# Windowed attention with a squared-ReLU feed-forward: from the fifth token tile on, tiles in pairs and Strassen's seven products in the first feed-forward matmul, with weights streamed from DRAM

## The chip, the core and the metric

The kernel runs on one core of a Trainium2 chip. The metric is the device time of one execution in microseconds; the kernel before takes 879.53 us, the median of 3 runs (877.98 to 879.83). Work is spread over TensorE (PE), VectorE (DVE), ScalarE (ACT), GpSimd (POOL) and SyncE (SP, which here only issues DMAs).

## The reference, cut to what matters

```
scores = q @ k.T / sqrt(64)            # 8 batches, 8 heads, 576 tokens, head size 64
scores = where(0 <= i - j < 64, scores, -1e9)
attn   = exp(scores - max); attn /= attn.sum() + 1e-9
x = (attn @ v), heads side by side     # 4608 tokens x 512
h = x @ w_in                           # 512 x 2048
g = max(h, 0) ** 2
out = g @ w_out                        # 2048 x 512
```

Weights arrive as 64-bit floats, so a weight row is twice as long in DRAM as in fp32.

## The kernel before

The 4608 tokens are cut into 12 tiles of 384. A feed-forward tile goes over 16 blocks `f` of 128 hidden units. For each block `mm1` (line 346) makes h, 128 units x 384 tokens, in 12 matmuls of 384 columns: 4 chunks of the model dimension, times 3 because fp32 accuracy is put together from two rounded halves (weight-hi x x-hi, weight-hi x x-lo, weight-lo x x-hi). `evac` then applies ReLU on ACT (op r), squares on DVE (p), rounds to the high half on ACT (g) and subtracts to the low half on DVE (G). `mm2` (line 387) follows two blocks later with 9 matmuls of 512 columns (3 token blocks x 3 halves) that add into three PSUM banks. One such step of mm1 and mm2 is the unit of the PE's work; a tile has 16.

The weights stay in SBUF for the whole run: `weight` (line 83) turns each 64-bit block into the two halves in the first stage, and all 16 blocks (`wparts`, 8 KB per partition each) stay there. Tiles 0 and 1 run interleaved in the first stage, by an order written out by hand (line 475), while weights load and convert. From line 541 on tiles 2 to 11 run one after another.

Attention for the next tile runs beside the feed-forward, in 36 sections of 4 query blocks, three to a tile. `section` (line 194) does one: S scores (PE), o and s copy and mask, z max, e and f exponentials (ACT), m normalise (POOL), X transpose (PE), x mask (DVE), V values (PE), H and Q the two halves of x. `step` (line 430) puts S of section i and V of section i-1 on the PE between an mm1 and an mm2. Queries and keys come as `raw` tiles: `load_qk` (line 114) issues 8 DMAs of 72 KB, whose runs in DRAM are 32 numbers long, into one of two buffers; `turn` (line 138) transposes a raw tile into `qk` on DVE, behind the last S that reads the old one, and the next load into that buffer waits for it. `load_v` (line 125) issues 64 KB DMAs into `vt`. Each engine takes its instructions strictly in the order in which the code emits them; all DMAs are issued by SP in one such queue. After a tile, ACT copies the three banks to `osb` (put Z, line 408) and SP writes them out (put W, line 410).

Of the kernel before, what the change touches and what calls it, by code (L numbers as in the profile page):

```python
# [20 lines left out]
NEG = -1.0e30  # L21


@with_exitstack
def window_attention_relu2_ffn(ctx: ExitStack, tc: tile.TileContext, q, k, v, w_in, w_out, out):
# [15 lines left out]
    wpool = ctx.enter_context(tc.tile_pool(name="wpool", bufs=NF))  # L41
    wst = ctx.enter_context(tc.tile_pool(name="wst", bufs=2))
    dram = ctx.enter_context(tc.tile_pool(name="dram", bufs=1, space=bass.MemoryType.DRAM))
    att = ctx.enter_context(tc.tile_pool(name="att", bufs=2))
    ffn = ctx.enter_context(tc.tile_pool(name="ffn", bufs=2))
    ps_a = ctx.enter_context(tc.tile_pool(name="ps_a", bufs=1, space=bass.MemoryType.PSUM))
    ps_h = ctx.enter_context(tc.tile_pool(name="ps_h", bufs=1, space=bass.MemoryType.PSUM))
    ps_o = ctx.enter_context(tc.tile_pool(name="ps_o", bufs=1, space=bass.MemoryType.PSUM))
# [65 lines left out]
    def load_qk(b, g):  # L114
        raw = raws[b, g] = att.tile([P, 2, S], F32, name="raw", bufs=2)
        for hd in range(2):
            for e in range(2):
                r = slice(32 * (2 * hd + e), 32 * (2 * hd + e) + 32)
                for n, x in enumerate((q, k)):
                    y = x[b, 4 * (g % 2) + 2 * (g // 2) + hd].rearrange("(t i) (e l) -> e i t l", i=32, e=2)[e]  # L120
                    sp.dma_start(raw[r, n].rearrange("i (t l) -> i t l", l=32), y)
# [3 lines left out]
    def load_v(b, t):  # L125
        vt = vts[b, t] = att.tile([P, 2, H // 2, D], F32, name="vt", bufs=5)
# [6 lines left out]
    def get_turned(b, d):  # L133
        if (b, d) not in turned:
            turned[b, d] = att.tile([P, 2, 2, S], F32, name="qk", bufs=2)
# [25 lines left out]
    def turn_first(b, t, d):  # L161
        n = tokens(b, t)
        early = b == 0 and 0 < 2 * t + d < 3
        ps = ps_o.tile([P, 2, 2, P], F32, name="oV" if early else "oT", bufs=2 if early else 1)
# [15 lines left out]
    def sel_tile(i):  # L180
        if i < 6 and i % 4 > 1:
            return extra[:, i % 2 * 512:(i % 2 + 1) * 512].rearrange("p (w h c) -> p w h c", w=SW, h=2)
        return att.tile([P, SW, 2, QB], F32, name="sel")

    def pt_tile(i):
        if i < 6 and i % 2:
            return extra[:, 1024:].rearrange("p (w q) -> p w q", q=P)
        return att.tile([P, 2 * SW, P], F32, name="pt", bufs=1)
# [5 lines left out]
    def section(op, i, eng=None):  # L194
# [3 lines left out]
        if op == "S":  # L198
            ps = ps_s[i] = ps_a.tile([P, 2, SW * P], F32, name="s_ps")
# [10 lines left out]
            nms[i] = att.tile([P, SW * 2], F32, name="nm", bufs=3)  # L210
            sums[i] = att.tile([P, SW * 2], F32, name="sums", bufs=3)
# [28 lines left out]
        elif op == "R":  # L240
            rs[i] = att.tile([P, SW * 2], F32, name="rs", bufs=3)
# [4 lines left out]
        elif op == "X":  # L246
            ps_t[i] = (ps_o.tile([P, SW * P], F32, name="oV", bufs=2) if i < 3 else
                       ps_a.tile([P, 2, SW * P], F32, name="v_ps")[:, 0]).rearrange("p (w q) -> p w q", w=SW)
# [8 lines left out]
        elif op == "V":  # L257

            ps = ps_x[i] = ps_a.tile([P, 2, SW * P], F32, name="v_ps")
# [17 lines left out]
        else:  # L277
            hi, lo = (x.rearrange("p (m d) x -> p m d x", d=2) for x in get_x(i // SPT))
# [43 lines left out]

    def get_x(t):
        if t not in xt:
            xt[t] = (ffn.tile([P, NPAIR, TT], F32R, name="xhi"), ffn.tile([P, NPAIR, TT], F32R, name="xlo"))
        return xt[t]
# [19 lines left out]
    def mm1(t, f):  # L346
        xhi, xlo = get_x(t)
        h_ps = ps_h.tile([P, TT], F32, name="h_ps")
        n = 0
        for kk in range(NK):  # L350
            for part, xx in ((0, xhi), (0, xlo), (1, xhi)):
                pe.matmul(h_ps, lhsT=wparts[f][:, 0, part, kk * P:(kk + 1) * P], rhs=in_turn(xx[:, kk, :]),  # L352
# [5 lines left out]
    def evac(op, n, eng=None):  # L358
        if op == "r":
            rg[n] = ffn.tile([P, TT], F32, name="r")  # L360
# [6 lines left out]
        elif op == "g":  # L367
            gs[n] = (ffn.tile([P, TT], F32R, name="ghi", bufs=3), ffn.tile([P, TT], F32R, name="glo", bufs=2))
# [15 lines left out]
    hs, rg, gs, accs = {}, {}, {}, {}  # L384


    def mm2(t, f, ghi, glo):
        if f == 0 and t == 1:
            accs[t] = [ps_a.tile([P, 2, SW * P], F32, name=x)[:, n] for x, n in (("s_ps", slice(0, 2)), ("v_ps", 0))]
            accs[t] = [accs[t][0][:, 0], accs[t][0][:, 1], accs[t][1]]  # L390
        elif f == 0:
            accs[t] = [ps_o.tile([P, DM], F32, name="oV" if tb else "oT", bufs=2 if tb else 1) for tb in range(NTB)]
        for tb in range(NTB):
            ts = slice(tb * P, (tb + 1) * P)
            for n, (gg, part) in enumerate(((ghi, 0), (ghi, 1), (glo, 0))):
                pe.matmul(accs[t][tb], lhsT=gg[:, ts], rhs=in_turn(wparts[f][:, 1, part, :]),  # L396
                          start=f == 0 and n == 0, stop=f == NF - 1 and n == 2)
            if f == NF - 1 and t != 1:
                for op in "ZW":
                    put(op, t, tb)  # L400
# [4 lines left out]
    def put(op, t, tb):  # L405
        if op == "Z":
            outs[t, tb] = wst.tile([P, DM], F32, name="osb", bufs=3)
            act.copy(by_half(outs[t, tb]), ordered(accs[t][tb]))
# [21 lines left out]
    def step(n, i, slot):  # L430
        if slot == 0:
            section("S", i)
            section("V", i - 1)
            evac("p", n)
            section("o", i)
            section("s", i)
            section("H", i - 1)
            evac("g", n)
            section("z", i)
            section("y", i, "d")  # L440
            section("e", i)
            section("Q", i - 1)
            evac("G", n)
            section("f", i)
            if i in loads:
                do_load_v(loads[i])
        elif slot == 1:
            section("k", i, "d")
            section("R", i)
            section("m", i)  # L450
# [5 lines left out]

# [126 lines left out]
```

## Time and profile before

| | |
|---|---|
| runs | 877.98 to 879.83 us, median 879.53 |
| profiled execution: span | 878.4 us (the page gives no other time for it) |
| PE busy | 860.0 us, 98% |
| weight loads of PE | 794.7 us, 90% |
| DVE busy | 452.0 us, 51% |
| ACT busy | 401.8 us, 46% |
| POOL busy | 50.1 us, 6% |
| DMA moved | 56.41 MB, 64 GB/s over the span |

In the profile a group's row has the line, the engine, the operation, the tiles (out<-in), the shape, the count, the busy time and the mean of one, and what ended the idle time before. A matmul's duration covers its pipeline, so the pace of the PE is read from the starts of its rows in time and not from their lengths. `SPq` rows are DMAs being issued. A row of the view by windows has the stretch and its length, then the busy time and the count of each engine, then the granted TensorE clock, the mean busy share of the 16 DMA engines and GB/s.

### The profile page before, as it was taken

Reading aid. Unit: us, or ns where it says so; the run is one execution under the profiler, and the core shown is the slowest. Engines: PE = TensorE matmul, PEld = TensorE weight load, DVE = VectorE, ACT = ScalarE, POOL = GpSimd, SP = SyncE. Lnnn points to the kernel's source line nnn. Section 1 sums busy time; section 2 is a strip of 40 time slices with the busy share of each in tenths; the row PEclk is TensorE's granted clock in tenths of the full one; section 3 lists DMA queues with packets and bytes.
Section 4 is the critical chain, followed back from the end, with each engine's and each line's share of the span. In section 5 each row is a group of like instructions: output and inputs, shape, how many; then the busy total and the mean of one; then the engine's idle time right before and its main releaser. Section 6 shows DMA issues by size and latency. Waiting matters only on the chain.

```text
span 878.4 us, 16976 instructions
## 1 busy us (share of the span) xinstructions
PE 860.0 (98%) x6946; PEld 794.7 (90%) x6946; DVE 452.0 (51%) x740; ACT 401.8 (46%) x1147; POOL 50.1 (6%) x70
## 2 busy tenths in 40 slices
PE   6799999999999999999999999999999999999998
PEld 5688998899999999999999999999999999999997
DVE  5799995754455444544455444453445544432222
ACT  5787875644344434434334444334434443432322
POOL 1210000210000000000000000000000000000000
PEclk9899999999999999999999999999999999999999
DMA  9989206460125002421033202141013200100100
GB/s 213 222 270 327 37 4 106 81 155 7 26 55 121 1 1 64 71 48 54 1 55 92 54 2 63 29 81 55 11 21 67 59 1 1 37 1 1 37 1 36
DMA packets 200302, 56.41 MB, mean 64 GB/s; under 512 B 185377, under 2 KB 193569, under 8 KB 200225
## 3 DMA queue, kind: packets, MB, share of 16 engines
q1 hardware_dynamic: 200224, 55.34, 27.4%
q8 instruction: 54, 0.88, 0.4%
q14 instruction: 24, 0.19, 0.1%
HBM read 45.88 MB, written 9.44 MB: 63 GB/s over the span
## 4 chain that ended last, share of the span: by engine, by line
PE 94%; SPq 3%; DMA 1%; ACT 1%; POOL 0%; DVE 0%; issue 0%; POOLq 0%
PE h_ps L352 42%; PE oV L396 26%; PE oT L396 14%; PE s_ps L208 3%; PE v_ps L272 3%; PE s_ps L396 2%; PE v_ps L250 1%; SPq L158 1%; PE v_ps L396 1%; SPq L130 1%; DMA w<-in_k_dram 1%; PE h_ps L500 0%; ACT sel L236 0%; SPq L80 0%; ACT r L361 0%
## 5 line engine op out<-in xcount | busy, mean ns | idle before, releaser
L352 PE MATMUL h_ps<-xhi,w 128*128 128x384 f32 x1536 | 407.0, 327 | 1.9 <-ACT r L361 1.4
L352 PEld LDWEIGHTS h_ps<-xhi,w 128*128 128x128 f32 x1536 | 275.2, 189 | 8.6 <-ACT r L361 3.3
L352 PE MATMUL h_ps<-xlo,w 128*128 128x384 f32 x768 | 250.6, 326 | 0.0
L361 ACT ACTIVATE r<-h_ps 128x384 f32<-128x384 f32 x192 | 93.6, 487 | 286.4 <-PE h_ps L352 285.7
L396 PE MATMUL oV<-w,ghi 128*128 128x512 f32 x704 | 209.5, 379 | 0.0
L366 DVE TENSOR_TENSOR r<-r 128x384 f32<-128x384 f32 x166 | 92.0, 554 | 165.4 <-ACT r L361 165.4
L371 DVE TENSOR_TENSOR glo<-r,ghi 128x384 fp32r<-128x384 f32 x192 | 107.8, 562 | 121.0 <-PE oV L396 82.0
L369 ACT CAST ghi<-r 128x384 fp32r<-128x384 f32 x192 | 98.8, 514 | 117.4 <-DVE r L366 115.4
L396 PEld LDWEIGHTS oV<-w,ghi 128*128 128x128 f32 x704 | 133.2, 189 | 18.8
L352 PEld LDWEIGHTS h_ps<-xlo,w 128*128 128x128 f32 x768 | 145.3, 189 | 4.8
L396 PE MATMUL oV<-w,glo 128*128 128x512 f32 x352 | 133.5, 379 | 0.0
L396 PE MATMUL oT<-w,ghi 128*128 128x512 f32 x352 | 110.2, 395 | 0.0
L236 ACT ACTIVATE sel<-sel,nm 128x64 f32<-128x64 f32 x272 | 90.8, 335 | 17.4 <-DVE nm L230 15.3
L396 PEld LDWEIGHTS oV<-w,glo 128*128 128x128 f32 x352 | 66.6, 189 | 9.4
L245 POOL TENSOR_TENSOR sel<-sel,rs 128x512 f32<-128x512 f32 x33 | 38.4, 1163 | 564.4 <-DVE rs L242 564.4
L396 PE MATMUL oT<-w,glo 128*128 128x512 f32 x176 | 66.8, 379 | 0.0
L254 DVE TENSOR_TENSOR pt<-v_ps,masks 128x1024 f32<-128x1024 f32 x31 | 38.0, 1224 | 46.8 <-PE v_ps L250 46.8
L396 PEld LDWEIGHTS oT<-w,ghi 128*128 128x128 f32 x352 | 59.0, 189 | 2.3 <-issue 0.2
L236 ACT ACTIVATION_READ_ACCUMULATOR sel<-sel,nm 128x1 f32 x272 | 50.9, 187 | 0.0
L140 DVE STREAM_TRANSPOSE qk<-raw 128x1152 f32<-128x1152 f32 x28 | 38.4, 1371 | 1.4 <-issue 1.4
L208 PE MATMUL s_ps<-qk 64*64 64x128 f32 (+1 forms) x1104 | 38.3, 276 | 0.1
L396 PEld LDWEIGHTS oT<-w,glo 128*128 128x128 f32 x176 | 33.3, 189 | 4.7
(80 smaller groups left out, 592.6 us busy)
## 6 DMA issues: line engine op xcount, KB each, us to landing
vt<-in_v_dram SPq DMA_DIRECT2D x144, 64.0 KB, 2.5
out_dram<-osb SPq DMA_DIRECT2D x36, 256.0 KB, 2.3
w<-in_moe_w_in_dram SPq DMA_DIRECT2D x16, 512.0 KB, 6.6
w<-in_moe_w_out_dram SPq DMA_DIRECT2D x16, 512.0 KB, 7.6
raw<-in_q_dram SPq DMA_DIRECT2D x112, 72.0 KB, 2.5
raw<-in_k_dram SPq DMA_DIRECT2D x112, 72.0 KB, 2.5
w<-in_q_dram SPq DMA_DIRECT2D x5, 256.0 KB, 4.6
w<-in_k_dram SPq DMA_DIRECT2D x5, 256.0 KB, 5.2
```

What stands on the lines that cost most here:

```text
L140: dve.transpose(get_turned(b, g // 2)[:, g % 2].rearrange("p n t -> p (n t)"), raw.rearrange("p n t -> p (n t)"))
L208: pe.matmul(ps[half * QB:(half + 1) * QB, j, w * P + c0:(w + 1) * P], lhsT=qk[r, 0, qb * QB:(qb + 1) * QB], rhs=qk[r, 1, k0:k0 + P - c0], ...
L236: act.activation(sels[i][:, w, hd], sels[i][:, w, hd], AF.Exp, bias=nms[i][:, n], scale=SCALE, accum_out=sums[i][:, n])
L245: (dve if eng == "d" else pool).tensor_tensor(p, p, rs[i][:, :, None].broadcast_to([P, SW * 2, QB]), ALU.mult)
L254: dve.tensor_tensor(pts[i].rearrange("p (w n) q -> p w n q", n=2), ps_t[i][:, :, None, :].broadcast_to([P, SW, 2, P]), masks.rearrange("p ...
L272: pe.matmul(ps[hd * D:(hd + 1) * D, j, q0:q0 + n * QB], lhsT=vts[b, kb // 2][r, kb % 2, 2 * d + hd, :], rhs=pts[i][r, n0:n0 + n, half * QB ...
L352: pe.matmul(h_ps, lhsT=wparts[f][:, 0, part, kk * P:(kk + 1) * P], rhs=in_turn(xx[:, kk, :]), start=n == 0, stop=n == 3 * NK - 1)
L361: act.activation(by_half(rg[n]), ordered(hs.pop(n)), AF.Relu)
L366: dve.tensor_tensor(rg[n], rg[n], rg[n], ALU.mult)
L369: act.copy(gs[n][0], rg[n])
L371: dve.tensor_tensor(gs[n][1], rg.pop(n), gs[n][0].bitcast(F32), ALU.subtract)
L396: pe.matmul(accs[t][tb], lhsT=gg[:, ts], rhs=in_turn(wparts[f][:, 1, part, :]), start=f == 0 and n == 0, stop=f == NF - 1 and n == 2)
```

## The change

The first stage stays, with three additions. Fixed buffers and PSUM banks replace the pools. Two more steps (tile 2, blocks 0 and 1) go into the hand-written order. Each converted weight block is also written to DRAM (`kept`, token B: 16 DMAs of 1 MB).

After the first stage the weight tiles are released and their space goes to new buffers. Weights come back from `kept` by DMA: `wi` blocks of 256 KB (half of an mm1 block, both roundings; 12 slots), `wo` blocks of 512 KB (an mm2 block; 8 slots). Tiles 2 and 3 run as before but with streamed weights: 30 more steps, two `wi` and one `wo` for each. In the same stretch the attention of tiles 4 and 5 is finished (9 sections instead of 6), and `mix` builds on POOL, for each pair p of blocks f, the four sums of weight quarters that Strassen's products need, and writes them to DRAM (`mixed`, 1 MB per p, 8 in all).

Tiles 4 to 11 run as 4 pairs j. The token half (first or second tile of the pair), the half of the model dimension and the block of a pair of f form the 2 x 2 x 2 cases. `operands` builds 7 combinations of the x quarters (POOL, DVE) and rounds each into two halves (ACT, DVE). Step s (8 per pair of tiles, 32 in all) does 7 products of 6 matmuls each where mm1 took 8 x 6: products 0 to 3 start four PSUM banks, products 4, 5 and 6 add into the banks of products 1, 2 and 3, after DVE has taken the first value out (`add` to v, u and g22). `second(s-2, x)` then does mm2 for four blocks f at once: 12 matmuls for each of 3 token blocks, whose result DVE adds to `part` in SBUF.

The order of the instructions on each engine from tile 2 on is no longer written by the loops but by `Plan`: each operation is entered with its engine, a cost, what it reads and writes and, for a DMA, a time to land; `in_order` lays them out by when they could start, the least late first, with PE in the order of entry. A DMA of weights is entered at 0.1 us of SP, `load_qk` (8 DMAs) at 0.8, one `load_v` at 0.4; transfers don't compete in it.

```
+NWI = 12
+NWO = 8
+NPLAIN = 4
...
+            elif op == "B":
+                sp.dma_start(kept[n], wparts[n].bitcast(F32))
...
+    wst.release()
+    wpool.release()
+    strm = ctx.enter_context(tc.tile_pool(name="strm", bufs=1, reuse_waits="tile"))
+    wi_t = [strm.tile([P, 2, 2, 2 * P], F32R, name=f"wi{n}") for n in range(NWI // 2)]
...
+        plan("sp", 0.1, by(sp.dma_start, wi[name][0].bitcast(F32), source), keys, [wi[name][1]], 3.5)
...
+        plan("sp", 0.1, by(sp.dma_start, wo[name][0].bitcast(F32), kept[f, :, 1]), [], [wo[name][1]], 5.0)
...
+                    plan("dve", 1.4, by(turn, b, g), [("raw", g % 2)], [("qk", g // 2, g % 2)])
...
+                    plan("sp", 0.8, by(load_qk, b, g), [], [("raw", g % 2)], 3.0)
...
+    def mix(p, n):
...
+        plan("sp", 0.1, by(sp.dma_start, mixed[p], mx.bitcast(F32)), ["mx0", "mx1"], [("mixed", p)], 4.0)
...
+    def product(s, n):
+        p = s % NP
+        kind = (0, "A11", 2, 3, "A12", "A22", 1)[n]
+        source = mixed[p, :, kind] if isinstance(kind, int) else block(2 * p + (kind[1] == "2"), int(kind[2]) - 1)
+        wi_fetch((s, n, "s"), source, [("mixed", p)] if isinstance(kind, int) else [])
+        w, w_key = wi[s, n, "s"]
+        if n < 4:
+            sums_of[s, n] = bank()
+        ps, key = sums_of[s, (0, 1, 2, 3, 1, 2, 3)[n]]
+        x = ops_x[n]
+
+        def do():
+            m = 0
+            for kk in range(2):
+                for part, xx in ((0, 0), (0, 1), (1, 0)):
+                    pe.matmul(ps[:, :TT], lhsT=w[:, part, kk * P:(kk + 1) * P], rhs=in_turn(x[:, xx, kk]),
+                              start=n < 4 and m == 0, stop=m == 5, skip_group_check=True)
+                    m += 1
...
+        if n == 0:
+            plan("act", 0.5, by(act.copy, sc, b[0][:, :TT]), [b[1]], ["sc"])
+        elif n == 1:
+            add(v, [kv], a[0][:, :TT], a[1], sc, "sc")
+        elif n == 2:
+            add(u, [ku], c[0][:, :TT], c[1], v, kv)
+        elif n == 3:
+            add(by_half(g22[0]), g22[1] + used, ordered(d[0][:, :TT]), d[1], ordered(u), ku)
+            square(g22, False, SQUARES[0])
...
+    def second(k, x):
...
+            for m in range(4):
+                for n, (gg, part) in enumerate(((hi, 0), (hi, 1), (lo, 0))):
+                    pe.matmul(ps, lhsT=gg[:, m // 2, m % 2], rhs=in_turn(w[m][0][:, part]),
+                              start=m == 0 and n == 0, stop=m == 3 and n == 2)
...
+            plan("dve", 0.72, by(dve.tensor_tensor, by_half(part), by_half(part), ordered(ps), ALU.add), [key], [kp])
...
     with tc.manual_schedule(engines={E.PE, E.DVE, E.Activation, E.Pool, E.SP}):
-        for t in range(2, NTILE):
-            for f in range(NF):
-                n = NF * t + f
-                m = min(f // 5, SPT - 1)
-                hs[n] = mm1(t, f)
-                evac("r", n)
-                step(n, SPT * (t + 1) + m + 1, f - 5 * m)
...
+        for do in plan.in_order():
+            do()
```

Two places of the new order matter below. The first is SP's queue at the end of the first stage, where it takes up the second stage. Before, the output of tile 0 (`osb`) is followed by loads of values and of queries and keys:

```order
L121 DMA raw<-in_q_dram 32x18x32
L121 DMA raw<-in_k_dram 32x18x32
L410 DMA out_dram<-osb 128x512 x3
L130 DMA vt<-in_v_dram 64x4x64 x6
L121 DMA raw<-in_q_dram 32x18x32
L121 DMA raw<-in_k_dram 32x18x32
```

Now the output of tile 0 stands ahead of every streamed weight (`wi_2017` is the slot of tile 2's block 2, which the PE wants next):

```order
L144 DMA raw<-in_q_dram 32x18x32
L144 DMA raw<-in_k_dram 32x18x32
L431 DMA out_dram<-osb 128x512 x3
L619 DMA wi_2017<-kept 128x2x256 x2
L619 DMA wo_2024<-kept 128x1024
L619 DMA wi_2018<-kept 128x2x256 x2
L619 DMA wo_2025<-kept 128x1024
L619 DMA wi_2019<-kept 128x2x256 x2
```

So from this row on weights, loads of attention, sums of weights and outputs share one queue, where before only loads and outputs did. Some 40 rows on, with the steps of tile 2 under way, a load of a `raw` tile is followed by weights and sums and then by the last DMAs of the second `raw` tile:

```order
L144 DMA raw<-in_k_dram 32x18x32
L619 DMA mixed<-g 128x2048
L619 DMA wo_2034<-kept 128x1024
L619 DMA wi_2018<-kept 128x2x256 x2
L144 DMA raw<-in_q_dram 32x18x32
L144 DMA raw<-in_k_dram 32x18x32
```

The second place is DVE's queue where those two tiles are turned. Before, the two turns of a section stand apart, several p and G (L366, L371) of the feed-forward between them:

```order
L140 STREAM_TRANSPOSE qk<-raw 128x1152
L366 TENSOR_TENSOR r<-r 128x384
L371 TENSOR_TENSOR glo<-r,ghi 128x384
L366 TENSOR_TENSOR r<-r 128x384
L371 TENSOR_TENSOR glo<-r,ghi 128x384
L254 TENSOR_TENSOR pt<-v_ps,masks 128x1024
L366 TENSOR_TENSOR r<-r 128x384
L371 TENSOR_TENSOR glo<-r,ghi 128x384
L140 STREAM_TRANSPOSE qk<-raw 128x1152
```

Now, in the step of tile 2 with the scores of section 13, both stand behind those scores and ahead of the next low half (L397):

```order
L392 TENSOR_TENSOR r<-r 128x384
L163 STREAM_TRANSPOSE qk<-raw 128x1152
L248 COPY_PREDICATED sel<-late,neg 128x128
L249 COPY_PREDICATED sel<-late,banks 128x384
L163 STREAM_TRANSPOSE qk<-raw 128x1152
L251 TENSOR_REDUCE nm<-sel 128x8
L397 TENSOR_TENSOR glo<-r,ghi 128x384
```

So two turns that can only start when their `raw` tiles have landed now stand in front of a low half that an mm2 waits for.

506 lines of the change are left out of this document (400 added, 106 removed).

## The prediction

> **What bounds the kernel now.** I read the page first, for the engines and the chain that ended last.
>
> ```profile
> PE 860.0 (98%) x6946; PEld 794.7 (90%) x6946; DVE 452.0 (51%) x740; ACT 401.8 (46%) x1147; POOL 50.1 (6%) x70
> PE 94%; SPq 3%; DMA 1%; ACT 1%; POOL 0%; DVE 0%; issue 0%; POOLq 0%
> DMA  9989206460125002421033202141013200100100
> ```
>
> The PE is 94% of the chain, DVE and ACT half idle, and DMA is nearly unused after the first 70 us. The timeline, late in the last tile, gives the pace of a step by starts of rows (12 matmuls of 384 columns, then 9 of 512):
>
> ```profile
> 800.59 0.33 PE L352 MATMUL h_ps<-xhi,w 128*128 128x384 f32 x1
> ...
> 802.54 0.60 PE L396 MATMUL oT<-w,ghi 128*128 128x512 f32 x2
> ...
> 804.49 0.33 PE L352 MATMUL h_ps<-xhi,w 128*128 128x384 f32 x1
> ```
>
> 802.54 - 800.59 = 1.95 us, so 0.1625 us a matmul of 384; the other 1.95 us are 0.2167 us a matmul of 512. A step is 3.90 us with nothing between its matmuls: the PE is at its own pace. Two more rows, the start of tile 2's first block and the last matmul, price an attention section:
>
> ```profile
> 192.12 0.33 PE L352 MATMUL h_ps<-xhi,w 128*128 128x384 f32 x1
> 874.33 0.38 PE L396 MATMUL oV<-w,glo 128*128 128x512 f32 x1
> ```
>
> 682.6 us lie between (with the last one's 0.38). They hold 160 mm1 and 162 mm2, 322 x 1.95 = 627.9 us, and 26 sections: 54.7 / 26 = 2.1 us each.
>
> **What the change takes away.** Per pair of blocks and pair of tiles, 48 matmuls of 384 become 42. There are 8 x 4 = 32 such cases: 192 matmuls x 0.1625 = 31.2 us of PE. The mm2 count is the same (36 of 512 a case), so is attention. A case takes 42 x 0.1625 + 36 x 0.2167 = 14.63 us.
>
> **What it adds on the engines that wait for it.** DVE's prices:
>
> ```profile
> L366 DVE TENSOR_TENSOR r<-r 128x384 f32<-128x384 f32 x166 | 92.0, 554 | 165.4 <-ACT r L361 165.4
> L254 DVE TENSOR_TENSOR pt<-v_ps,masks 128x1024 f32<-128x1024 f32 x31 | 38.0, 1224 | 46.8 <-PE v_ps L250 46.8
> L228 DVE TENSOR_REDUCE nm<-sel 128x8 f32<-128x512 f32 x34 | 23.3, 684 | 1.0
> L226 DVE COPY_PREDICATED sel<-late,s_ps 128x512 f32<-128x512 int32 x20 | 14.8, 738 | 10.6 <-ACT sel L216 10.4
> ...
> L140 DVE STREAM_TRANSPOSE qk<-raw 128x1152 f32<-128x1152 f32 x28 | 38.4, 1371 | 1.4 <-issue 1.4
> L289 DVE TENSOR_TENSOR xlo<-v_ps,xhi 128x512 fp32r<-128x512 f32 x20 | 13.6, 681 | 2.6 <-ACT xhi L287 2.5
> L245 POOL TENSOR_TENSOR sel<-sel,rs 128x512 f32<-128x512 f32 x33 | 38.4, 1163 | 564.4 <-DVE rs L242 564.4
> ```
>
> A case needs on DVE 5 adds and 2 squares of 384 (7 x 0.55 = 3.9 us) and 3 low halves and 3 sums of 512 (6 x 0.68 = 4.1): 8.0 us of 14.63. With a section (1.22 + 0.68 + 0.74 = 2.6 us, and at most two turns, 2.7) it is 13.3 of 16.7, 80%. DVE fits, if it isn't held up. The tight place is product 4, which overwrites the bank of product 1: product 1 ends at 2 x 0.98 = 2.0 us of the case, the add to v takes 0.55, product 4 starts at 3.9, so there is 1.3 us of room. Product 5 and 6 have the same. I put nothing on it, with a rival below. POOL's 6 adds of `mix` and two of its low halves come to about 9 us at 1163 ns per 512 numbers, 8 times: off the path, as long as the last `mixed` is written by product 6 of the first case.
>
> **What it adds on DMA, where the sum is decided.** The prices come from stretches in which SP issued only one kind. From 64 to 84 us weights were loaded (runs of 1 and 4 KB), from 88 to 92 raw tiles, from 194 on values:
>
> ```profile
> 64.00:84.00 20.00, 18.84 (x103) 17.24 (x102) 18.69 (x23) 13.87 (x21) 0.00 (x0) 1.00 1.06 375
> 88.00:92.00 4.00, 4.00 (x24) 3.76 (x23) 3.76 (x6) 3.73 (x6) 0.00 (x0) 1.00 0.85 137
> 194.00:197.50 3.50, 3.50 (x21) 3.26 (x20) 1.12 (x2) 1.00 (x2) 0.00 (x0) 1.00 0.52 145
> ...
> 90.24 0.50 SPq L121 DMA_DIRECT2D raw<-in_q_dram  x1
> 90.79 0.50 SPq L121 DMA_DIRECT2D raw<-in_k_dram  x1
> 193.49 3.96 SPq L130 DMA_DIRECT2D vt<-in_v_dram  x6
> ...
> raw<-in_q_dram SPq DMA_DIRECT2D x112, 72.0 KB, 2.5
> out_dram<-osb SPq DMA_DIRECT2D x36, 256.0 KB, 2.3
> ```
>
> Weights move at 375 GB/s with the 16 engines full (share 1.06). A raw load comes every 0.55 us (90.24 to 90.79) with the engines 0.85 busy: 0.46 us of all 16 engines for 72 KB, which at 375 GB/s would be 0.20; its short runs make it dear. A value load comes every 0.66 us at 0.52: 0.34 us.
>
> Between the end of the first stage and the end of the second Strassen case, SP's queue now holds, counted in the new order: 78 `wi` (64 for tiles 2 and 3, 14 for the products), 40 `wo`, 8 writes of `mixed` and 6 outputs, which are 20.4 + 21.0 + 8.4 + 1.6 = 51.4 MB, 137.0 us at 375 GB/s; 64 raw loads (29.4 us) and 36 value loads (12.2 us). Together 178.6 us of full DMA engines.
>
> The PE needs for the same stretch 30 steps x 3.90 + 9 sections x 2.1 + 14 products x 0.975 + S and V of one section, about 1.8: 117.0 + 18.9 + 13.7 + 1.8 = 151.4 us. So the transfers are the longer side by far, and the queue is in order: nothing can be brought forward.
>
> It also begins late. The output of tile 0 stands ahead of the first weights, and this is how such an output ran before:
>
> ```profile
> 191.07 0.57 ACT L408 COPY osb<-oT 128x512 f32<-128x512 f32 x1
> 191.67 1.72 SPq L410 DMA_DIRECT2D out_dram<-osb  x3
> ```
>
> SP is through with it at 193.39, 1.27 us after the PE was (192.12, above). Before, that hid behind the next step; now the next step's weights stand behind it. With 1.27 us, 178.6 us of transfers, 1.6 us from the end of a transfer to its landing (2.3 for 256 KB less 0.7 of moving) and the last product, 1.0, the second case ends 182.5 us after the first stage's last matmul, 31.1 us later than the PE alone would. I expect the first 3 to 4 us of it at once (the PE idle from the last matmul of tile 0), 5 to 10 us near section 13 and again near section 17, where turns wait on DVE for raw loads behind weights and hold up the low halves of the steps, and the rest in the first two cases. These don't add to the sum: while the PE waits for one of them DMA moves on, and slots are free in time.
>
> From the third case on DMA has room: a case moves 7 x 0.26 + 2 x 0.52 = 2.9 MB, 7.7 us of 14.6, and with a section's loads some 14 of 16.7. There the PE should run at its pace.
>
> The Trainium skill, DMA: Bandwidth & Descriptors, section Specifications, gives a limit of about 358 GB/s of HBM to a core. By that the 137.0 us would be 143.5, estimated, and the loss 6.5 us more. The 375 GB/s over 20 us in the row above speaks against it, and I go by the row.
>
> The clock can add a little. The windows from 30 us on show that a thin stretch of PE work is followed by a granted clock of a half:
>
> ```profile
> 30.00:32.00 2.00, 1.05 (x8) 0.75 (x8) 1.47 (x3) 0.45 (x2) 0.43 (x2) 1.00 1.36 147
> 32.00:36.00 4.00, 3.15 (x15) 2.92 (x16) 3.26 (x4) 3.60 (x12) 0.00 (x0) 0.60 0.64 119
> 36.00:40.00 4.00, 4.00 (x67) 3.66 (x70) 1.74 (x3) 2.45 (x11) 1.28 (x2) 0.54 1.07 318
> ```
>
> The clock lost 4 x 0.40 + 4 x 0.46 = 3.4 us of PE there. After the waits inside the stretch this costs nothing, since DMA decides; after the last one, when the PE leads again, it costs between 0 and 3.4 us: I take 1.7. The Trainium skill, TensorE: Matmul & The Clock Gate, section The HAM clock gate, tells of half the clock after an idle window of about 3.4 us; the rows agree in the size and show it after less than 3 us of thin work.
>
> The first stage should not change: 16 writes of 1 MB, 2.8 us each at 375 GB/s, go into about 75 us in which the row of DMA shares above is mostly 0 to 4 tenths, and only loads with time to spare stand behind them. Below nothing I see no reason; above it 2 us. The tail gains or loses nothing: the last sum on DVE (0.68) takes the place of ACT's copy (0.57).
>
> **The sum.** 878.4 - 31.2 (matmuls) + 31.1 (DMA in the second stage) + 1.7 (clock) = 880.0 us of span. The runs' median is 1.1 us above the span of the profiled execution, so 881 us in their terms: no change to the measure, by two large terms that cancel. A difference of 0.2%, 1.8 us, is about what a measurement can tell here.
>
> **The ends of the unknown cost.** What raw and value loads take beside large transfers no row shows. From below: the engines overlap their short runs fully and only bytes count, 64 x 0.20 + 36 x 0.17 = 18.9 instead of 41.6 us, 22.7 us less: 858. From above: SP's issue is never hidden (0.55 and 0.66 us), 64 x 0.09 + 36 x 0.32 = 17.3 us more: 898. I take the middle, the engines' own time, as the 88 to 92 us row has it.
>
> **Rivals.** First, the weights stream unseen: slots for six steps ahead keep the PE fed, and only the start costs, 1.3 + 0.7 + 1.6 us for the first block, 3.6 in all: 878.4 - 31.2 + 3.6 + 1.1 = 852; with part of the short runs hidden, 852 to 870. For it speaks the share of 1.06, which shows that packets overlap; against it that 178.6 us would have to shrink to 155, which weights alone at an even higher rate would not do. Chance 0.20.
>
> Second, slower, by DVE in the product chain. If v comes out of its bank more than 1.3 us late, product 4 waits, and so with u and g22. From 0.03 us a case on (1 us in all) that decides the sign of the sum, since the two large terms cancel. With one turn in front of v in each section case and DVE at 80%, 0.5 us a case on average, 16 us: 897. For it speak the strict order of DVE and two turns of 1371 ns in one case; against it that in most cases nothing but a max (0.68) stands in front of v, and that 1.3 us covers it. Chance 0.18.
>
> Third, that SP waits for a buffer whose reader, POOL in `mix`, is late itself (9 us for each p, and everything behind it in the queue is held): 0.04, and 890 or more.
>
> The forecast has 0.58, with a range of its own of 870 to 891 (5% of 137 us to both sides, and the clock). Of it 0.22 lie under 0.2% faster, 0.14 within, 0.22 slower. So faster 0.22 + 0.20 = 0.42, same 0.14, slower 0.22 + 0.18 + 0.04 = 0.44. Range 860 to 898: the first rival's lower half (0.10) and the ends of the others (0.10) lie outside.
>
> **What would show it.** In the changed kernel's profile: windows of the second stage from some 200 to 355 us with a DMA share near 1 throughout and the PE at 80 to 85%, after it a PE near 100% and a DMA share of 0.5 to 0.6; in the waits, mm1 of the streamed weights and the products held by DMA of `wi`, and DVE's turns by `raw`; a gap of 3 to 4 us behind the last matmul of tile 0; 192 fewer matmuls. I am wrong if the DMA share stays under 0.8 there and PE still waits, if a DMA-full second stage takes under 165 us, or if the PE loses more than 5 us in cases 3 to 32.

## The result, and the profile after

The changed kernel takes 935.0 us (median of 4 runs, 930.97 to 937.05) against 879.68 of the kernel before: a ratio of 1.063, 95% interval 1.060 to 1.066. It is 55 us slower, outside the range that was given. (Of one run below, costs_half_weights, the profiled execution was a disturbed one; its undisturbed times are used and its trace is not.) The engines, the chain and the DMA shares on its page:

```profile
PE 846.6 (91%) x6754; PEld 774.5 (83%) x6754; DVE 589.3 (63%) x870; ACT 406.9 (44%) x1119; POOL 196.7 (21%) x210
PE 77%; DMA 10%; SPq 5%; POOL 3%; ACT 1%; DVE 1%; issue 1%; POOLq 0%; DVEq 0%; ACTq 0%
DMA  9989959489999698699799878898967646686521
```

There are 192 matmuls fewer, and the PE's part of the chain fell from 94% to 77%. The profiled execution (span 933.6) splits into three stretches; here the second and the third, with the clock, the DMA share and GB/s at the end of the row:

```profile
198.52:418.85 220.33, 158.82 (x1342) 143.25 (x1342) 98.73 (x139) 79.12 (x250) 85.48 (x76) 0.85 0.88 252
418.85:929.87 511.02, 510.71 (x3845) 472.25 (x3843) 338.15 (x536) 201.00 (x556) 90.65 (x90) 1.00 0.72 206
```

From the first product (418.85) on the PE is busy in 510.7 of 511.0 us at full clock: Strassen's part runs at the PE's pace and its 31.2 us are saved. Before that stand 30 mm1, 32 mm2 and 9 sections. At 1.95 us and 2.4 us (how the section comes to 2.4 is told below) they need 62 x 1.95 + 9 x 2.4 = 142.5 us; they took 220.3. What the PE waited for in them (columns: the wait, its sum, how often, the longest):

```profile
PE banks L272 <- POOL sel L268: 38.3, 4, 20.6
PE banks L378 <- ACT r L387: 18.5, 6, 10.2
PE banks L378 <- DMA wi<-kept: 4.6, 1, 4.6
```

61.4 us of waits; the other 16.4 of the 77.8 are the clock, granted at 0.85 over the stretch (the PE is busy for 158.8 us with work of 142.5). For its own weights, the third row, the PE waits only once, at the start. The first two rows lead to `mix`. Here is the longest wait of the second row, on ACT and on the PE:

```profile
224.54 1.04 ACT L619 CAST g<-g 128x1024 fp32r<-128x1024 f32 x1 [11.06 <-POOL g L619]
225.50 0.48 ACT L387 ACTIVATE r<-banks 128x384 f32<-128x384 f32 x1
226.03 3.65 PE L378 MATMUL banks<-x,wi 128*128 128x384 f32 x12 [10.21 <-ACT r L387]
```

The next mm1 writes the bank that the ReLU (r, L387) has to read first. In ACT's strict queue the copy of `mix` (L619, `g<-g`) stands ahead of that ReLU; the copy waited for POOL, and POOL for the `wi` of blocks 0 and 1 of tile 2. Only `mix` reads these two in this stretch, since their mm1 ran in the first stage. So the PE stood still for weights that it did not need.

The longest wait of all, by rows in time. PE:

```profile
283.96 0.38 PE L420 MATMUL banks<-wo,glo 128*128 128x512 f32 x1
304.99 1.11 PE L272 MATMUL banks<-ident,sel 128*128 128x128 f32 x4 [20.64 <-POOL sel L268]
```

POOL, whose queue has `mix` ahead of the multiply (L268) that the transposes wait for:

```profile
302.67 1.26 POOL L619 TENSOR_TENSOR g<-wi 128x512 f32<-128x512 f32 x1 [32.59 <-DMA wi<-kept]
303.89 1.04 POOL L268 TENSOR_TENSOR sel<-sel,nm 128x512 f32<-128x512 f32 x1
```

SP, which issues the DMAs:

```profile
274.82 1.71 SPq L619 DMA_DIRECT2D wi<-kept  x2
276.58 10.28 SPq L153 DMA_DIRECT2D vt<-in_v_dram  x8
286.95 0.55 SPq L144 DMA_DIRECT2D raw<-in_q_dram  x1
...
296.69 0.50 SPq L144 DMA_DIRECT2D raw<-in_k_dram  x1
297.29 0.96 SPq L619 DMA_DIRECT2D wi<-kept  x2
298.34 0.43 SPq L619 DMA_DIRECT2D wo<-kept  x1
298.86 0.90 SPq L619 DMA_DIRECT2D wi<-kept  x2
299.85 0.82 SPq L619 DMA_DIRECT2D wo<-kept  x1
308.05 0.36 SPq L619 DMA_DIRECT2D wi<-kept  x1
```

For 20.7 us, from 276.58 to 297.29, SP issues 8 value loads, 16 raw loads and one `wo`, and no `wi`. The weights that POOL waits for stand behind them, and the PE waits for POOL. The value loads, half of the 20.7 us, are wanted by the V at 311, soon after the stop. The first of the raw tiles is read at 344, by this row of DVE:

```profile
344.47 1.36 DVE L163 STREAM_TRANSPOSE qk<-raw 128x1152 f32<-128x1152 f32 x1
```

So raw loads that were wanted 55 us later stood ahead of weights that `mix` wanted at once. The PE itself reads the block issued at 297.29 only at 328.24, in its fifth mm1 after the stop; the four blocks before it had all been issued by 276.53. Here too it is `mix`, ahead in POOL's queue, that turns a late load into a stop of the PE. Traced back in this way, row by row, some 54 of the 61.4 us stand behind an operation of `mix` on POOL or ACT, the 14.1 us before the transposes of section 17 among them. After that SP has its slots full and issues nothing for some 7 us (300.7 to 308.05). Two windows, inside the wait and behind it:

```profile
284.18:304.99 20.81, 0.17 (x2) 0.01 (x1) 0.56 (x1) 0.00 (x0) 2.26 (x2) 0.57 0.93 192
305.00:310.00 5.00, 5.00 (x20) 4.56 (x24) 1.23 (x1) 0.02 (x1) 4.17 (x5) 0.50 0.30 96
```

The DMA share is 0.30 at the moment when the PE works again, at half clock.

In the first stage ACT, DVE and PE stand still once:

```profile
93.00 14.07 SPq L519 DMA_DIRECT2D kept<-w  x10
104.42 1.04 ACT L127 CAST w<-a 128x1024 fp32r<-128x1024 f32 x1 [10.35 <-DMA kept<-w]
105.90 3.98 PE L378 MATMUL banks<-x,w 128*128 128x384 f32 x12 [7.64 <-ACT r L387]
```

A cast of new weights goes into the buffer of block 2, which used to be free by then; now a write to `kept` still has to read it. The stage ends at 198.52. Before, at 192.12, the PE had done the same blocks and one section more, so the stage is 192.12 - 2.4 = 189.7 there, and 8.8 us longer now. The ledger: 8.8 + 77.8 - 31.2 = 55.4; the spans differ by 55.2.

### The profile page after: what moved, and what is told of

Read it like the earlier page. It is cut to its first block, busy times and chain, and to the rows that moved or that the text cites. A ratio compares the mean times of both kernels' runs of the same rounds, so it can differ in the third digit from the quotient of the medians.

```text
span 933.6 us, 17902 instructions
## 1 busy us (share of the span) xinstructions
PE 846.6 (91%) x6754; PEld 774.5 (83%) x6754; DVE 589.3 (63%) x870; ACT 406.9 (44%) x1119; POOL 196.7 (21%) x210
## 4 chain that ended last, share of the span: by engine, by line
PE 77%; DMA 10%; SPq 5%; POOL 3%; ACT 1%; DVE 1%; issue 1%; POOLq 0%; DVEq 0%; ACTq 0%
PE banks L881 27%; PE banks L812 24%; PE banks L378 11%; PE banks L420 9%; DMA wi<-kept 5%; PE banks L231 3%; PE banks L294 3%; POOL g L619 2%; SPq L144 2%; PE banks L272 1%; DMA mixed<-g 1%; SPq L181 1%; DMA kept<-w 1%; SPq L153 1%; SPq L619 1%
## 5 line engine op out<-in xcount | busy, mean ns | idle before, releaser
L881 PE MATMUL banks<-wo,hi 128*128 128x512 f32 x768 | 229.8, 381 | 0.0
L619 POOL TENSOR_TENSOR g<-g 128x384 f32<-128x384 f32 (+2 forms) x112 | 105.6, 948 | 328.0 <-ACT g L619 311.1
L881 PEld LDWEIGHTS banks<-wo,hi 128*128 128x128 f32 x768 | 143.1, 189 | 18.1
L881 PE MATMUL banks<-wo,lo 128*128 128x512 f32 x384 | 145.5, 379 | 0.0
L812 PE MATMUL banks<-x,wi 128*128 128x384 f32 x768 | 135.3, 326 | 0.0
L812 PEld LDWEIGHTS banks<-x,wi 128*128 128x128 f32 x768 | 126.5, 189 | 0.1
L619 ACT CAST hi<-g 128x512 fp32r<-128x512 f32 x96 | 59.4, 620 | 131.1 <-PE banks L881 129.0
L812 PE MATMUL banks<-xb,wi 128*128 128x384 f32 x576 | 105.9, 329 | 0.0
L812 PEld LDWEIGHTS banks<-xb,wi 128*128 128x128 f32 x576 | 94.7, 189 | 2.0
L378 PE MATMUL banks<-x,wi 128*128 128x384 f32 x360 | 75.0, 365 | 23.1 <-ACT r L387 18.5
L619 DVE TENSOR_TENSOR part<-part,banks 128x512 f32<-128x512 f32 x72 | 49.4, 687 | 69.5 <-PE banks L881 69.5
L378 PEld LDWEIGHTS banks<-x,wi 128*128 128x128 f32 x360 | 68.2, 214 | 26.9 <-ACT r L387 20.8
L619 DVE TENSOR_TENSOR lo<-g,hi 128x512 fp32r<-128x512 f32 x96 | 65.8, 688 | 31.3 <-ACT hi L619 31.3
L378 PE MATMUL banks<-x,w 128*128 128x384 f32 x408 | 74.8, 334 | 9.5 <-ACT r L387 9.1
L881 PEld LDWEIGHTS banks<-wo,lo 128*128 128x128 f32 x384 | 72.6, 189 | 10.3
L387 ACT ACTIVATE r<-banks 128x384 f32<-128x384 f32 x64 | 31.3, 489 | 105.4 <-PE banks L378 104.8
L272 PE MATMUL banks<-ident,sel 128*128 128x128 f32 x136 | 22.2, 289 | 39.3 <-POOL sel L268 38.6
```

The source lines that it names most:

```text
L272: pe.transpose(ps_t[i][:, w], sels[i][:, w].rearrange("p h c -> p (h c)"), ident)
L378: pe.matmul(h_ps, lhsT=weights(kk, part), rhs=in_turn(x[xx][:, kk // 2, kk % 2]), start=n == 0, stop=n == 3 * NK - 1)
L387: act.activation(by_half(rg[n]), ordered(hs.pop(n)), AF.Relu)
L619: return lambda: op(*args)
L812: pe.matmul(ps[:, :TT], lhsT=w[:, part, kk * P:(kk + 1) * P], rhs=in_turn(x[:, xx, kk]), start=n < 4 and m == 0, stop=m == 5, skip_group_c ...
L881: pe.matmul(ps, lhsT=gg[:, m // 2, m % 2], rhs=in_turn(w[m][0][:, part]), start=m == 0 and n == 0, stop=m == 3 and n == 2)
```

## The experiments

Theories: (Q) the order in SP's queue, loads that are not wanted yet ahead of loads that are; (E) the sum of the DMA engines' time, which is longer than the PE's; (P) POOL's queue, `mix` ahead of the sections. The copy of `mix` on ACT was in none of them, and no run moves `mix` alone. In the table the stage ends and stretches are read from each trace; the columns should be 189.7, 142.5 and 511.0 if nothing waited.

| run | us | first stage ends | to the first product | from there to the end |
|---|---|---|---|---|
| changed kernel | 935.0 | 198.5 | 220.3 | 511.0 |
| late_writes | 950.9 | 206.7 | 224.1 | 511.0 |
| writes_before_raw | 929.3 | 195.3 | 216.5 | 511.3 |
| writes_of_2_to_4_later | 923.1 | 188.6 | 217.5 | 511.4 |
| norm_on_dve | 928.8 | 199.2 | 215.6 | 511.1 |
| no_small_loads | 890.3 | 196.2 | 174.8 | 511.9 |
| no_mix | 901.5 | 197.8 | 180.9 | 519.4 |
| half_weights | 911.1 | 197.1 | 196.7 | 511.1 |
| costs_as_measured | 916.1 | 196.7 | 185.1 | 529.9 |
| all_three | 915.5 | 195.5 | 185.9 | 527.4 |
| costs_half_weights | 880.7 | | | |
| tile3_reversed | 901.8 | 198.8 | 186.1 | 511.0 |
| tile3_reversed_costs | 886.8 | 199.2 | 168.4 | 515.0 |
| tile3_reversed_costs_writes | 886.6 | 197.8 | 170.5 | 515.4 |
| reversed_costs_writes_later | 878.7 | 187.9 | 168.6 | 513.9 |
| reuse_more | 874.3 | 189.6 | 167.8 | 511.4 |
| reuse_more_norm_on_dve | 874.2 | 188.9 | 167.9 | 511.0 |

### The first stage

```
-  p6a B0 M7 ... G7 B1 M8 ... d7 g8 B2 M9 ...
+  p6a M7 ... G7 M8 ... d7 g8 M9 ...  l15 B0 B1 ... O21 B2 B3 ... O22 B4 B5 ...
```

> The 16 writes of kept weights come after the last weight block is converted, two per step, instead of from block 0 on. If the 10.35 us in which ACT's cast (L127) stands at 94 to 104 us is the wait for the third of these writes, the PE's 7.6 us gap there goes and the time falls by 7 to 9 us, to 926 to 928; the rival, that DMA traffic as such slows the conversion, expects the gap to move to where the writes now are: 0 to -3 us. If the writes now push the first raw loads back, up to +4.

+16 us, more than either expected. The stop at 98 us is gone, but the writes now stand in front of raw and value loads, and sections wait for those (14.1 us of waits between 130 and 207 us). The stage ends 8.2 us later.

```
-  l4 q0 Q5 ... g4 q1 c6 ... g10 c9 a10 B4 M11
+  l4 Q5 ... g4 c6 ... g10 c9 a10 B4 q0 q1 M11
```

> In the order of the first stage the first two raw loads (32 DMAs, 77 to 93 us on SP) come after the first five writes of kept weights and not ahead of them; nothing else is changed. The cast of a later block goes into the buffer of block 2, 3 or 4 and so waits for that block's write. If that is the gap of 7.6 us, it goes: -6 to -9 us, 926 to 929. If the writes cost their traffic wherever they stand, as when they were put late (+16), the time stays or rises: 0 to +10.

-5.7. The wait became smaller and moved to an earlier cast, since the buffer of block 2 is now given away earlier too:

```profile
92.70 1.04 ACT L127 CAST w<-a 128x1024 fp32r<-128x1024 f32 x1 [5.83 <-DMA kept<-w]
```

```
-  ... B2 M9 ... B3 M10 ... B4 M11 ... h13 c14
+  ... M9 ... M10 ... M11 ... h13 B2 B3 B4 c14
```

> Only the writes of blocks 2, 3 and 4 move, behind the conversion of block 13, so that no cast takes their buffers early; the other writes stay where they were. If the reuse of these buffers is the whole of the first stage's loss, the gap at 98 to 106 us goes and the first stage ends 7 to 9 us earlier: 926 to 928. If the traffic of the writes costs as well, 0 to -4: 931 to 935.

-11.9, more than expected. The stage ends at 188.6, where it did before, 9.9 us earlier; the second stretch is 2.8 us shorter besides. In the windows from 80 to 120 us the PE is busy throughout:

```profile
80.00:100.00 20.00, 20.00 (x109) 18.71 (x108) 19.90 (x22) 16.47 (x23) 0.00 (x0) 1.00 0.97 285
100.00:120.00 20.00, 19.87 (x107) 18.11 (x106) 19.90 (x23) 15.84 (x23) 0.00 (x0) 1.00 1.01 419
```

At a DMA share of 0.97 and 1.01 the PE does not wait: the traffic of the writes costs nothing here, the reuse of three buffers did.

### Which of the three theories

```
-                plan("pool", 1.2, by(section, "m", i), [r], [sel])
+                plan("dve", 0.7, by(section, "m", i, "d"), [r], [sel])
```

> Only the multiply that normalises a section (L268, m) goes from POOL to DVE, so no section stands behind mix on POOL. If POOL's queue is the cause of the 38.6 us that the PE waits for it, these go, with 6 or more us at half clock: -38 to -46 us, 889 to 897. If mix is itself only waiting for weights that the next block needs as well, the wait moves from the transposes to mm1 (wi<-kept): 0 to -6 us, 929 to 935.

-6.2. The PE's waits in the second stretch:

```profile
PE banks L378 <- ACT r L387: 32.4, 5, 16.4
PE banks L272 <- DVE sel L268: 15.4, 2, 13.3
PE banks L378 <- DMA wi<-kept: 4.9, 1, 4.9
```

38.3 us at the transposes became 15.4, and 18.5 at mm1 became 32.4. The longest of these, 16.4 us, ends with these rows of ACT:

```profile
312.32 1.04 ACT L619 CAST g<-g 128x1024 fp32r<-128x1024 f32 x1 [18.88 <-POOL g L619]
313.27 0.48 ACT L387 ACTIVATE r<-banks 128x384 f32<-128x384 f32 x1
```

The section no longer stands behind `mix`, but two mm1 later a ReLU does, on ACT, and so the PE waits for the same weights as before. The run took only one of the two ways from `mix` to the PE away. That it gained only 6.2 us does not say that `mix` ahead in a queue costs little.

```
-            if b < B:
+            if b < B and i > 18:
...
-                if 1 < b < B:
+                if 1 < b < B and i <= 18:
+                    raws[b, g] = raw_t[:, g % 2]
+                elif 1 < b < B:
                     plan("sp", 0.8, by(load_qk, b, g), [], [("raw", g % 2)], 3.0)
```

> From the third section of tile 4's attention to the last section of tile 5's, the loads of raw queries and keys and of values are left out (the old contents are used). Weights, mixed writes and outputs stay, 52 MB or 137 us at 375 GB/s beside 158 us of PE. If transfers cause the loss, by their sum or by their order, nearly all of it goes: -55 to -70 us, 865 to 880. If POOL's chain or the slots that mix holds cause it, the 20 us waits stay: -5 to -25 us, 910 to 930.

-44.7. Less than expected under Q or E: 32 us of the 77.8 stay. The wait at the start of the stretch is there as before, without any small load in it, and again behind the copy of `mix`:

```profile
221.97 1.04 ACT L619 CAST g<-g 128x1024 fp32r<-128x1024 f32 x1 [10.98 <-POOL g L619]
223.46 3.64 PE L378 MATMUL banks<-x,wi 128*128 128x384 f32 x12 [10.14 <-ACT r L387]
```

So small loads ahead in SP's queue are not the whole of it. The long stop at section 13 is gone: its transposes now wait 1.8 us.

```
-        if n % 2 and (f // 2 % 2 == t % 2):
-            mix(f // 2, n - 1)
-        source = mixed[p, :, kind] if isinstance(kind, int) else block(...)
+        source = block(2 * p + kind % 2, kind // 2) if isinstance(kind, int) else block(...)
```

> The mixed weight quarters are neither built nor written; the products that read them load quarters of the kept weights instead, so the products' loads are as many and as large. Out go 8 writes of 1 MB, two 1 us copies of ACT and all of mix on POOL, and weight slots no longer wait for POOL. By engine time, 8.4 MB at 328 to 375 GB/s: -22 to -30 us, 905 to 913. If it is mostly the slots that POOL holds: -35 to -55 us, 880 to 900. If neither, 0 to -10.

-33.5, between the two expectations. The PE's waits in the second stretch are now these:

```profile
PE banks L294 <- DMA vt<-in_v_dram: 11.7, 2, 6.5
PE banks L378 <- DMA wi<-kept: 4.5, 1, 4.5
PE banks L272 <- POOL sel L268: 3.7, 1, 3.7
PE banks L378 <- ACT r L387: 3.5, 1, 3.5
```

23.4 us instead of 61.4, and the stops of 10.2, 14.1 and 20.6 us are gone. The stretch is 39.4 us shorter; 8.4 come back in the first Strassen cases. Value loads now hold the PE directly. How much of the gain is the place of `mix` in the queues, how much its 8 MB of writes and how much the slots that POOL no longer holds, this run alone does not tell.

```
+        some = slice(0, 2 if wi_n[0] <= NWI else 1)
-        plan("sp", 0.1, by(sp.dma_start, wi[name][0].bitcast(F32), source), ...
+        plan("sp", 0.1, by(sp.dma_start, wi[name][0][:, some].bitcast(F32), source[:, some]), ...
```

> Of every streamed weight block after the first 12 and the first 8 only the high half is loaded (128 KB for 256, 256 KB for 512): the same DMAs in the same order with about 18 MB less of the 61 that move between the first stage and the end of the second case. If engine time is the limit there, 209 us of it fall to about 157, no longer above the PE's 158: -45 to -60 us, 875 to 890. If the order and the count of issues on SP are the limit (small loads and early output weights in front of urgent ones), the waits stay for the greater part: -10 to -25 us, 910 to 925.

-23.9, as Q expected. Some 50 us of engine time are gone, and the big stop is still there behind the same 24 small loads and the same operation of `mix`: 26.6 us of waits at L272, the longest 16.0. E alone does not hold.

```
-        plan("sp", 0.1, by(sp.dma_start, wi[name][0].bitcast(F32), source), keys, ...
+        plan("sp", 0.7, by(sp.dma_start, wi[name][0].bitcast(F32), source), keys, ...
...
-                    plan("sp", 0.8, by(load_qk, b, g), [], [("raw", g % 2)], 3.0)
+                    plan("sp", 4.3, by(load_qk, b, g), [], [("raw", g % 2)], 3.0)
```

> Only the planner's costs of SP change, to what the DMAs take in the trace: 0.7 us for 256 KB, 1.4 for 512 KB, 2.8 for a mixed write, 4.3 for load_qk, 2.6 for load_v. The same DMAs in another order. If the order (small loads in front of weights) makes the loss, it falls by 20 to 45 us, to 890 to 915. If the DMA work as such is the limit (0.89 of 236 us is 209 us of full engines, against 158 that the PE needs), it falls by 0 to 12 us: 923 to 935.

-18.9: the same loads in another order. But the plan lays out every engine by these costs, and `mix` moved too: in the changed kernel its eight copies on ACT stand behind the 35th, 38th, 40th, 42nd, 47th, 51st, 56th and 60th ReLU of the run, and here behind the 38th, 43rd, 48th, 53rd, 56th, 58th, 61st and 64th. The PE now waits mostly for its own `wi`, 20.9 us in nine waits. The run shows what the costs in the plan are worth; it does not divide that between the order of the loads and the place of `mix`. The second stretch is 35.2 us shorter and no wait in it is longer than 7.7 us, but 18.9 come back in the first cases, where the transfers that were put off still have to be made:

```profile
196.66:381.75 185.09, 152.20 (x1341) 136.06 (x1341) 99.80 (x138) 78.64 (x249) 87.65 (x75) 0.95 0.90 260
381.75:450.00 68.25, 61.26 (x571) 56.25 (x569) 40.63 (x69) 31.41 (x106) 12.19 (x13) 0.95 0.94 262
```

With the plan mended the engines are at 0.90 and 0.94, which fits E as the limit now. The next run relieves both (these costs, and half of each streamed block).

> SP's order as in the run with measured costs (916), and of each streamed weight block after the first 12 and 8 only the high half. If two limits act, the order and the engine time, then with both relieved (about 193 - 50 = 143 us of engines under 158 of PE) nearly all of the second stage's loss goes: -34 to -46 against 916, 870 to 882. If the order is the only limit and the rest is latency or slots, halving the bytes adds little to 916: 905 to 916.

-54.3 (880.7). The plan's costs alone gave 18.9, bytes alone 23.9, both 54.3, more than their sum: each hides behind the other.

> SP's costs as measured (-19 alone), the normalising multiply on DVE (-6 alone), and the first raw loads behind the first five writes. If the three losses add: -30 to -35 us, 900 to 905. If the order already frees POOL in time, the middle one adds nothing: 906 to 912. It beats the kernel before only if the transfers fit under the PE, which 193 us of engine time against 158 speaks against.

-19.5, as good as the costs alone (the multiply on DVE as above, the writes as in writes_before_raw). The other two changes add nothing here; the run does not show why. The first stage is only 1.2 us shorter than with the costs alone.

### Versions with fewer loads

Tile 3 may take its blocks in any order. From 15 down to 0 it finds 6 `wi` and 8 `wo` blocks where tile 2 left them, and the first pair finds 8 `wo` of tile 3.

```
+            if last and f < NWI // 2:
+                wi[n, h] = wi[3 * NF - 1 - f, h]
+            elif last:
+                wi_fetch((n, h), block(NF - 1 - f, h), 2 * ((3 - f) % 6) + h)
...
+        if last and f < NWO:
+            wo[n] = wo[3 * NF - 1 - f]
...
+                if j == 0 and group < 2:
+                    wo[j, f] = wo[4 * NF - 1 - f]
```

> Correct variant: tile 3 takes its blocks from 15 down to 0, so that 6 wi blocks and 8 wo blocks of tile 2 are used again without a load, and 8 wo blocks of tile 3 by the first pair: 11.5 MB less (some 35 us of full engines at 171 us for 56 MB). The planner's costs are the changed kernel's. By engine time -25 to -35, 900 to 910. By the order of the queue, the first stall of 20 us stays (it lies in tile 2) and the one of 14 us in tile 3 goes: -14 to -22, 913 to 921.

-33.2, as E expected. But it is not bytes alone: half_weights took some 50 us of engine time away and gained 23.9. Here the stops of 20.6 and 14.1 us are gone as well (the longest wait is 9.3), since the first `mix` of tile 3 now finds its block where tile 2 left it.

> The reversed tile 3 with SP's costs as measured. Engine time 193 - 35 = 158 us, equal to the PE's need; if both limits act, 916 less 25 to 35: 881 to 891. If reversal gives what the order gave already, 905 to 916.

-48.2, nearly the sum of the two alone (33.2 + 18.9 = 52.1). The PE's waits in the second stretch are 17.8 us, none over 5.7.

> The same with the first two raw loads behind the first five writes of kept weights in the first stage (-5.7 alone): 4 to 7 us less than with the reversed tile and costs alone, 875 to 886; below the kernel before only at the lower end.

No gain over the run before. The first stage ends only 1.4 us earlier, since an earlier cast waits instead (as in writes_before_raw), and the second stretch is 2.1 us longer.

> The reversed tile 3 with measured costs (886.8) and the writes of blocks 2 to 4 later. If the first stage's gain is kept through the transfers of the second stage: 878 to 881, equal to the kernel before. If the second stage is held by its own transfers from a start that is no earlier: 883 to 887.

878.7, a ratio of 0.999 (0.997 to 1.001) to the kernel before: the first stage's 8 us are kept when the cast waits for nothing.

```
+        if s < 2 and isinstance(kind, str):
+            wi[s, n, "s"] = wi[NPLAIN * NF - 1 - 2 * p - (kind[1] == "2"), int(kind[2]) - 1]
-            sp.dma_start(out[t * TT + tb * P:...
+            (act if t == 0 else sp).dma_start(out[t * TT + tb * P:...
```

> As the one before, and six more weight loads of 256 KB left out (the products of the first two cases read the wi blocks that tile 3 left), and the outputs of tile 0 issued by ACT, so that the first fetch of weights is not behind them. By engine time -5 us, by the start -1.7 us: 872 to 876, below the kernel before. If what is left is order and latency: 878 to 882.

874.3, ratio 0.995 (0.993 to 0.997). The run makes two changes, fewer loads and the outputs of tile 0 on ACT, and does not tell them apart.

> As the one before, with the normalising multiply on DVE. POOL's chain was worth 6 us in the changed kernel, where weights came late; with them in time I expect 0 to -3 us against the run before. If DVE becomes late in the Strassen cases, +2 to +10.

874.2, ratio 0.994 (0.992 to 0.996): 0.6% below the kernel before and 6.5% below the changed one. The multiply on DVE adds nothing that can be told. Its second stretch in the PE's waits:

```profile
PE banks L378 <- DMA wi<-kept: 9.0, 4, 3.7
PE banks L420 <- DMA wo<-kept: 4.0, 1, 4.0
PE banks L378 <- ACT r L387: 3.8, 2, 2.0
PE banks L272 <- DVE sel L268: 1.9, 1, 1.9
```

18.7 us of waits, none over 4 us. The stretch is 167.9 us, still 25 above the PE's 142.5.

## Why the prediction was wrong

**The anchor.** It took the row at 192.12 for tile 2's first block. It is the third: 34 mm1 and 32 mm2 lie before it. So 318 x 1.95 = 620.1 of the 682.6 us are matmuls, and a section is 62.5 / 26 = 2.4 us, not 2.1. And 32 mm2, not 30, belong to the second stage. Both put the PE's need up to the end of the second case at 158 us instead of 151.4. With that the prediction would have forecast a gain of some 5 us, and been further off: this error did not cause the miss.

**Right:** the 31.2 us of matmuls; the Strassen cases at the PE's pace (0.3 us of waits in 511, so the second rival, v late from its bank, did not happen); that the second stage is where the change loses; the price of the small loads, nearly. Between the changed kernel and no_small_loads the engines' time up to the end of the second case falls from 235.9 x 0.89 = 210 to 190.3 x 0.87 = 166 us, for 64 raw and 36 value loads: 44 us, where 41.6 was worked out. The rows of the two, and of the second what its queue moved in MB:

```profile
198.52:434.39 235.87, 174.36 (x1489) 158.47 (x1489) 108.07 (x157) 86.33 (x275) 88.33 (x80) 0.86 0.89 259
```

```profile
196.18:386.50 190.32, 166.79 (x1489) 152.69 (x1489) 109.79 (x157) 86.50 (x275) 90.00 (x80) 0.94 0.87 288
```

```profile
q1 hardware_dynamic: 31022, 54.53, 86.9%
```

**Right place, by luck:** stops near section 13 and near section 17. They are there, at the transposes of just these sections (20.6 and 14.1 us), but not by way of DVE's turns, which in this stretch wait for no `raw` tile. The way is `mix` on POOL.

**The step that failed** is the one on `mix`: "off the path, as long as the last `mixed` is written by product 6 of the first case." It gave `mix` a deadline and asked only when it ends, not what stands behind it in POOL's and ACT's queues while it waits for weights. Some 54 of the PE's 61.4 us of waits stand behind it. Without `mix` the waits are 23.4 us and the stretch is 39.4 us shorter. With this step falls the sentence "These don't add to the sum: while the PE waits for one of them DMA moves on, and slots are free in time." They do add. During the stop of 20.8 us the engines were busy (0.93), but while the PE stood, its slots stayed full and SP stopped behind it, and the share then fell to 0.30. Over the 235.9 us the engines were idle for some 26.

Behind both lies the plan. The text ahead of the prediction names the costs, 0.1 us of SP for a DMA of weights and 3.5 us to land; the prediction took from it only that "nothing can be brought forward". In such a plan SP is hardly ever busy. So each load goes into the queue when its buffer falls free (how soon it is wanted decides only between loads that can start within 0.05 us of each other, `NEAR` in the code), and `mix` goes into the queues of POOL and ACT as if its weights were there. With the costs as measured the time falls by 18.9 us, and by 30 with half the weights (911.1 to 880.7). How much of that is the loads and how much `mix`, no run shows.

**Mis-sized terms.** The engines' time was 210 us, not 178.6, so some 31 of the 53 us by which this stage ran over (235.9 for 182.5) are in the transfers' own time and the rest is idle time. The small loads were nearly right; the run almost without them took 166 us for 54.5 MB (some 3 more than counted, fetched ahead for the third case and on), 3.0 us per MB where 375 GB/s means 2.7. The clock cost 16.4 us and not 1.7: it was counted once, but the PE's long stops were each followed by a stretch at half clock (0.50 from 305 to 310 us above). The Trainium skill, TensorE: Matmul & The Clock Gate, section The HAM clock gate, gives half the clock after an idle window of about 3.4 us. The rows agree (0.57 over the stop of 20.81 us, 0.50 behind it), and the prediction had the rule and applied it to the last wait only. The first stage, bounded at 2 us, cost 8.8, by a buffer's new reader that the change's diff shows and the prediction did not follow.

**The third rival,** at 0.04, was nearest: it named `mix` as the one that holds others up. But it had the wait the other way round. SP waited only 5.2 us for POOL; POOL and ACT waited for SP's loads, and the PE for them.

Open: how the 33.5 us of no_mix divide between the place of `mix`, its transfers and held slots; how the gain of the plan's costs divides between the order of the loads and the place of `mix`; and what makes the last 25 us of the best version's second stretch; its waits are 18.7, none over 4 us, at a mean DMA share of 0.91.

## What to carry to other kernels

When an engine's bound turns into a transfer's, look at the order of the queue as well as at its sum: ask of every load ahead of an urgent one when it is read. Do the same for the engines that compute: work with no hurry that waits for a late load holds everything behind it in a strict queue, and the engine named in a wait may itself stand behind such work. A list scheduler orders only what its costs make scarce, so DMAs with a cost near nothing are laid down by when a buffer falls free, and what reads them as if they had landed. And a new reader of a buffer (a write-back) delays whoever takes that buffer next, in a stage that the change does not seem to touch.

## What the hardware showed

An engine share near 1 says nothing of the bytes: weights moved at 382 GB/s at a share of 1.06 and raw tiles at 166 at 1.23. The writes of `kept` ran at 421 GB/s here and at 419 over 20 us in writes_of_2_to_4_later (above), faster than the loads in these rows:

```profile
215.70:226.00 10.30, 0.12 (x1) 0.00 (x0) 0.00 (x0) 1.46 (x3) 5.74 (x7) 0.65 1.06 382
295.00:300.00 5.00, 0.00 (x0) 0.00 (x0) 0.00 (x0) 0.00 (x0) 0.00 (x0) 0.50 1.23 166
98.10:105.90 7.80, 0.17 (x1) 0.00 (x0) 0.41 (x1) 1.45 (x3) 0.00 (x0) 0.79 1.00 421
```

The Trainium skill, DMA: Bandwidth & Descriptors, section Anatomy of one DMA — SWDGE (gpsimd) path, says that a DMA waits for semaphores on the engine that issues it, before it is dispatched. The trace agrees for SP, which from 198 to 434 us waited 23.2 us for slots that the PE's mm1 held, with every other load behind:

```profile
SPq L619 <- PE banks L378: 23.2, 16, 7.6
SPq L619 <- POOL g L619: 5.2, 5, 2.9
```
